# A transformer block in fp32 halves: the first token block's modulation, keys and queries reordered, and the feed-forward's norms and divisions moved to other chunks

## The chip, the core and the metric

The kernel runs on one core of one Trainium2 chip. A core has five engines, each with an instruction queue of its own: TensorE (PE, with weight loads shown as PEld), VectorE (DVE), ScalarE (ACT), GpSimd (POOL) and SyncE (SP), which here only issues DMAs. The metric is the device time of one execution in microseconds.

## The reference

One layer on x of 2048 tokens by 512 features, with a conditioning vector c of 512:

```
mod = silu(c) @ w_mod                       # six vectors of 512: sa, ca, ga, sb, cb, gb
h = layernorm(x) * (1 + ca) + sa
x = x + ga * (softmax attention of h, 32 heads of 16, wqkv, wo)
h = layernorm(x) * (1 + cb) + sb
x = x + gb * (gelu(h @ w1 + b1) @ w2 + b2)  # w1: 512 x 1792
```

## The kernel before

Wherever an fp32 product is needed, both operands are split into a rounded part (hi) and the rest (lo), and three matmuls are added up: hi·hi, lo·hi and hi·lo. `mm3` (L290 to L302) writes that order out for the four feature chunks of 128: eight matmuls that need only the hi of the second operand, then four that need its lo.

Tokens come in four blocks of 512 (b), features in four chunks of 128 (fc). Everything is issued in the order of the program text (`manual_schedule`), each engine in order; a wait on one instruction holds all behind it on that engine.

**Start.** SP issues the loads in this order: c, the four tiles of x's block 0, two whole 1 MB pieces of w_mod (1+ca and sa, L187, `load_wm` L137), block 0's share of the key and query weights (`load_w(0)`), and from L494 on the value weights, x's block 1 and the next weights. DVE takes mean and variance of block 0's rows (L236) and normalises them (L278). TensorE runs 22 products with the identity while it waits for data (`keep_warm`, L506, L510), then the modulation matmuls with ca (`mod_part`, L200), 12 of the 16 transposes of block 0, the matmuls with sa, and the last four transposes. ACT copies the modulation row out of PSUM (L213), four small matmuls turn it into columns (`mod_cols`, L216), DVE puts them into `modc`. `evac` (L260) then makes each feature chunk of hT: ACT scales and shifts the transposed chunk into an fp32 tile h (L262), DVE rounds it to hi (L263), DVE or POOL subtracts to give lo (L264). `split_w(0)` (L164) splits the first weights on DVE and POOL, `split_w(4)` the value weights on ACT, DVE and POOL.

**Loop over blocks** (L535 to L563). For block b: statistics of block b+1 (`ln1`), x of block b+2 is loaded, keys then queries of head group 0 are projected (`proj_qk`, 12 matmuls each into one PSUM bank of the ring "sc", four banks), block b+1's rows are normalised, `V_A[b][0]` value tiles are projected (`proj_v`, 12 matmuls each), block b+1 is transposed and evacuated, `V_A[b][1]` more value tiles, and for b < 2 the matmuls of the next modulation pair. After that come the remaining projections with row maxima beside them, and attention proper.

**Feed-forward** (from L869). 56 steps: four token blocks (qb) by 14 chunks of the 1792 features. Step i issues on each engine, in this order: the load of step i+4's weights, their split for step i+2 (`split_f`, L726: DVE rounds w1, POOL subtracts, DVE rounds w2, POOL subtracts), `ffn1(i)` (12 matmuls; ACT gelu, ACT rounds ghi, DVE subtracts glo, L906 to L910), `ffn2(i-1)` (12 matmuls into four accumulator banks, L927, the third of them needs glo of step i-1), and then what a table `plan` holds for this step. At the end of a token block `ffn2` also ends the block: DVE multiplies each accumulator by gb into one of three tiles y (L932), POOL adds it to x2 (L936; in the last block DVE does), SP stores. The table places, by step number: the attention output's division for blocks 2 and 3 (`o_norm`: a load of the reciprocals, then on DVE a multiply L781, a rounding L782 and a subtraction L783 for each feature chunk), the output projections (`o_proj`, 12 matmuls and a DVE add), and the second layer norm (`put_ln2`: statistics, `rows(t)` with two DVE instructions for a tile, L816 and L817, and transposes with four instructions a pair of chunks on ACT and DVE). In the loop's last two steps `ffn2` is left to the end (L1012 to L1017).

Of the kernel before, what the change touches and what calls it, by code (L numbers as in the profile page):

```python
# [7 lines left out]
F32 = mybir.dt.float32  # L8
# [16 lines left out]
NB = 4  # L25
# [27 lines left out]
def block_kernel(ctx: ExitStack, tc: tile.TileContext, x, wqkv, wo, w1, b1, w2, b2, c, w_mod, out):  # L53
# [28 lines left out]
    def bank():  # L82
        return ring("sc")
# [48 lines left out]
    sel_b = apool.tile([P, 2, P], F32, name="sel_b")  # L132
    ones = apool.tile([P, 2 * S // P], F32, name="ones")
    gp.memset(ones, 1.0)

    wm_r = w_mod.rearrange("(k p) n -> p k n", p=P)

    def load_wm(i, slot):
        sy.dma_start(halves[1][slot], wm_r[:, :, i * D : (i + 1) * D])
        return halves[1][slot]  # L140

    def x_tile(b, t):
# [10 lines left out]
    def load_w(k):  # L153
# [7 lines left out]
                sy.dma_start(raw[:, i], wq_r[:, i, 2 * D :])  # L161
        raws[k] = raw

    def split_w(k):  # L164
        raw = raws.pop(k)
        if k < 4:
            t = wslots[k % 2].rearrange("p a (b n) -> p (a b) n", n=P).rearrange("p (h w k) n -> p h w k n", h=2, w=2)
            for w in (1, 0):
                if k == 0:
                    ve.tensor_copy(t[:, 0, w], raw[:, w])  # L170
                elif k > 1:
                    gp.tensor_copy(t[:, 0, w], raw[:, w])
                else:
                    ac.activation(t[:, 0, w], raw[:, w], AF.Copy)
                eng = ve if k == 0 and w else gp
                eng.tensor_tensor(t[:, 1, w], raw[:, w], t[:, 0, w].bitcast(F32), op=ALU.subtract)
            w_hi[k], w_lo[k] = t[:, 0], t[:, 1]
        else:
            w_hi[k], w_lo[k] = vslots
            for i in range(KC):  # L180
                ac.activation(w_hi[k][:, i], raw[:, i], AF.Copy)
                eng = gp if i % 2 else ve
                eng.tensor_tensor(w_lo[k][:, i], raw[:, i], w_hi[k][:, i].bitcast(F32), op=ALU.subtract)
# [4 lines left out]
    load_w(0)  # L188


    ac.activation(s_c, c_c, AF.Exp, scale=-1.0)
# [8 lines left out]
    def mod_part(ps, i, wm):  # L200

        for k in range(KC):
            te.matmul(ps[32 * k : 32 * (k + 1)], s_m[:, i, k], wm[:, k], start=i == 0, stop=i == 1)

    def mod_rows(wms):
        ps = bank()
# [1 line left out]
            mod_part(ps, i, wms[i])  # L208
        return mod_copy(ps)

    def mod_copy(ps):
        r = apool.tile([P, D], F32, tag="h32", name="mrow", bufs=3)
        ac.activation(r, ps, AF.Copy)  # L213
        return r

    def mod_cols(v, r):  # L216

        ps = bank()
        for fc in range(KC):
            te.matmul(ps[:, fc * 2 : fc * 2 + 2], r[:, fc * P : (fc + 1) * P], sel[:, :2], start=True, stop=True)  # L220
        p2 = ps[:, : 2 * KC].rearrange("p (f i) -> p f i", i=2)
        ve.tensor_scalar(modc[:, v, :, 0], p2[:, :, 0], 1.0, None, op0=ALU.add)
        ve.tensor_copy(modc[:, v, :, 1], p2[:, :, 1])

    def mod_store(r):

# [77 lines left out]

    st = [ac]

    def proj_qk(b, k, w, fill=()):
        hi, lo = hT[b]
        ps = bank()
        mm3(ps, [w_hi[k][:, w, i] for i in range(KC)], [w_lo[k][:, w, i] for i in range(KC)],  # L310
            [hi[:, i] for i in range(KC)], [lo[:, i] for i in range(KC)], fill)
        parts = tpool.tile([P, 2, TB], FR, tag="parts", name="parts", bufs=5)
        pair = w and k < 2
        if k or pair and b % 2 == 0:
            raw = tpool.tile([P, TB], F32, tag="raw", name="raw", bufs=3)
            ac.activation(raw, ps, AF.Copy)
            if pair:
                k2[b % 2] = raw
        if k:
            gp.tensor_copy(parts[:, 0], raw)  # L320
            gp.tensor_tensor(parts[:, 1], raw, parts[:, 0].bitcast(F32), op=ALU.subtract)
        else:
            ac.activation(parts[:, 0], ps, AF.Copy)
            ve.tensor_tensor(parts[:, 1], ps, parts[:, 0].bitcast(F32), op=ALU.subtract)
        if pair and b % 2:
            pm = [tpool.tile([P, TB], F32, tag="pm", name="pm", bufs=1), k2[0]]
            pmh = [tpool.tile([P, 2, TB], FR, tag="parts", name="pmh", bufs=5) for _ in range(2)]
            if not k:
                for i, op in enumerate((ALU.add, ALU.subtract)):
                    ve.tensor_tensor(pm[i], ps, k2[0], op=op)  # L330
                    ac.activation(pmh[i][:, 0], pm[i], AF.Copy)

        def pair_store():
            for i in range(2):
                t0 = (b - 1 + i) * TB
# [18 lines left out]
    def proj_v(b, t, fill=()):  # L354
        hi, lo = hT[b]
        ps = bank()
        sl = slice(t * P, (t + 1) * P)
        mm3(ps, [hi[:, i, sl] for i in range(KC)], [lo[:, i, sl] for i in range(KC)],
            [w_hi[4][:, i] for i in range(KC)], [w_lo[4][:, i] for i in range(KC)], fill, late_b=False)
# [131 lines left out]
        return [] if left[u] else [max_rows(u)]  # L491


    load_w(4)  # L494
    load_x(1)
    load_w(1)
    sy.dma_start(one_d.rearrange("a (p f) -> (a p) f", p=P // 2), ones)
    xn = ln1(0)()
    for t in vst:
        gp.memset(t[:, :, 4 * VW :], 0.0)  # L500
        for j in range(4):
            gp.memset(t[:, :, j * VW + DH], 1.0)
    split_w(0)
    warm = bank_pv()

    def keep_warm(n):  # L506
        for i in range(n):
            te.matmul(warm[:, :P], ident, ident, start=True, stop=True)

    keep_warm(NWARM)  # L510
    ps = bank()
    mod_part(ps, 0, wms[0])
    ev = ln1_t(0, xn, lambda: mod_part(ps, 1, wms[1]))
    mrow = mod_copy(ps)
    keep_warm(5)
    mod_cols(0, mrow)
    ev()
    split_w(4)
# [12 lines left out]
    for b in range(NB):  # L531
# [6 lines left out]
            load_qm(0)  # L538
        if b + 1 < NB:
            rows = ln1(b + 1)  # L540
        if b + 2 < NB:
            load_x(b + 2)
        proj(proj_qk, b, 0, 1)
        if b == NB - 1:
            st[0] = sy
            rest()
            rest, st[0] = lambda: None, ac
            build_k(kts[0], kpm_d[0], 0, 0, 2 * TB)
            split_w(1)
            load_w(2)  # L550
        else:
            xn = rows()
        proj(proj_qk, b, 0, 0)
        if b == NB - 1:
            mod_store(mrow)
            break
        if b == 1:
            mod_cols(1, mrow)
        for _ in range(V_A[b][0]):
            proj(proj_v, *vitems.pop(0))  # L560
        ev = ln1_t(b + 1, xn)
        ev()
        for _ in range(V_A[b][1]):  # L563
# [421 lines left out]
    put_ln2(2, (0, 13), epool)  # L985
    put_ln2(3, (1, 11), fpool)
    for i in range(NI):
        qb, f = divmod(i, NF)
        if i + 4 < NI:
            load_f(i + 4)  # L990
        if i + 2 < NI:
            split_f(i + 2)
        ffn1(i)
        if i and i < NI - 2:
            ffn2([i - 1])
        for fn in plan.get((qb, f), []):
            fn()
    ffn2([NI - 3])
    ffn2([NI - 2, NI - 1])
    close(fcm)  # L1000
    close(kcm)

# [25 lines left out]
```

## Time and profile before

| | us |
|---|---|
| median of 3 runs (lowest, highest) | 1750.32 (1749.57, 1751.95) |
| the profiled execution's own time | 1751.07 |
| its span, first to last instruction | 1749.3 |
| PE busy | 1732.7 (99% of the span) |
| DVE, ACT, POOL busy | 1396.8, 1350.3, 320.2 |
| granted TensorE clock, mean | 0.998 |
| first block up to the first keys of block 1 | 0 to 41.45 |
| projections and row maxima, attention | to 1392 |
| feed-forward, from its first output projection | 1391.79 to the end |

Times on the trace are counted from the span's start. A row of the timeline gives start, duration, engine, line, operation, output and inputs with partitions and elements, and in brackets how long the engine had been idle and what ended it. An fp32 matmul counts as two instructions ("x44" for 22). A matmul row's duration includes its way through the array; the next one starts after about 0.227 us, which is the price of one 128x512 matmul in a stream.

### The profile page before, as it was taken

The numbers are of one execution on the slowest core, as the hardware profiler recorded it, in microseconds if no ns is written. First come the engines' busy times: TensorE is split into PE (matmuls) and PEld (weight loads), VectorE is DVE, ScalarE is ACT, GpSimd is POOL, SyncE is SP. The second block draws the span as 40 slices with busy tenths as digits, with TensorE's granted clock in tenths as the row PEclk, the third lists the DMA queues.
The fourth block names the chain that finished last, engine by engine and source line by source line (L and its number), as shares of the span: only waits on it lengthen the run. The fifth ranks groups of instructions, "written<-read, shape, count | busy, mean of one in ns | idle before, by whom it ended". The sixth has DMA issues, their size and how long they took to land.

```text
span 1749.3 us, 28886 instructions
## 1 busy us (share of the span) xinstructions
PE 1732.7 (99%) x10554; PEld 900.7 (51%) x10554; DVE 1396.8 (80%) x2553; ACT 1350.3 (77%) x2580; POOL 320.2 (18%) x347
## 2 busy tenths in 40 slices
PE   8999999999999999999999999999999999999998
PEld 6765554434343434343434343334333478788887
DVE  6579999898888888888888888888885295837453
ACT  3478888999999999999999999999999632212222
POOL 3205431010000000000000000000012154536462
PEclk9999999999999999999999999999999999999999
DMA  7777657611300501500510110111023164423331
GB/s 267 251 156 177 152 126 147 111 36 41 68 23 17 84 23 23 87 23 23 82 29 23 39 36 23 39 26 33 23 65 106 31 194 120 133 72 118 99 121 49
DMA packets 124098, 144.15 MB, mean 82 GB/s; under 512 B 38930, under 2 KB 72722, under 8 KB 122004
## 3 DMA queue, kind: packets, MB, share of 16 engines
q1 hardware_dynamic: 120644, 135.55, 31.6%
q10 hardware_dynamic: 3312, 6.76, 1.0%
q8 instruction: 83, 1.36, 0.4%
q14 instruction: 59, 0.48, 0.1%
HBM read 106.37 MB, written 35.87 MB: 81 GB/s over the span
## 4 chain that ended last, share of the span: by engine, by line
PE 93%; DVE 3%; DMA 1%; issue 1%; POOL 1%; SPq 0%; ACT 0%; ACTq 0%; DVEq 0%; POOLq 0%
PE pv L696 29%; PE mx L429 20%; PE sc L300 15%; PE sc L863 13%; PE mx L927 5%; PE mx L446 5%; PE pv L927 2%; PE sc L803 1%; PE mx L803 1%; DVE glo L910 0%; DMA wmod<-in_w_mod_dram 0%; POOL w2l L734 0%; DMA rb<-rden 0%; PE sc L257 0%; PE mx L257 0%
## 5 line engine op out<-in xcount | busy, mean ns | idle before, releaser
L864 ACT ACTIVATE p<-sc 128x512 f32<-128x512 f32 x2048 | 1054.7, 613 | 38.1 <-PE sc L863 12.5
L431 DVE TENSOR_REDUCE mxs<-mx 128x1 f32<-128x512 f32 x1472 | 927.7, 684 | 112.3 <-PE sc L863 87.3
L696 PE MATMUL pv<-p,vg 128*32 128x512 f32 x4096 | 546.0, 605 | 0.0
L863 PE MATMUL sc<-qst,kq 50*128 50x512 f32 x1024 | 284.2, 435 | 0.0
L863 PE MATMUL sc<-qst,kt 50*128 50x512 f32 x1024 | 282.0, 431 | 0.0
L429 PE MATMUL mx<-kq,qmx 48*128 48x512 f32 x768 | 261.7, 428 | 0.2
L429 PEld LDWEIGHTS mx<-kq,qmx 48*128 48x128 f32 x768 | 122.6, 184 | 228.6 <-DVE mxs L431 209.3
L429 PE MATMUL mx<-kt,qmx 48*128 48x512 f32 x704 | 240.0, 428 | 0.0
L906 ACT ACTIVATE g<-sc,b_c 128x512 f32<-128x512 f32 x56 | 38.6, 690 | 238.7 <-PE sc L300 230.6
L429 PEld LDWEIGHTS mx<-kt,qmx 48*128 48x128 f32 x704 | 113.4, 184 | 208.4 <-DVE mxs L431 190.6
L455 DVE CUSTOM_DVE_ANT_0 cp<-mx,cp 128x512 f32<-128x512 f32 x288 | 182.5, 687 | 25.9 <-PE mx L446 23.2
L468 POOL CAST m<-mn 128x16 fp32r<-128x16 f32 x32 | 6.3, 196 | 1018.4 <-DVE mn L462 1018.4
L696 PEld LDWEIGHTS pv<-p,vg 128*32 128x32 f32 x4096 | 81.1, 108 | 180.5 <-issue 168.9
L452 ACT ACTIVATE cp<-mx 128x512 f32<-128x512 f32 x288 | 151.6, 604 | 27.9 <-PE mx L446 27.0
L863 PEld LDWEIGHTS sc<-qst,kq 50*128 50x128 f32 x1024 | 125.5, 185 | 32.2 <-ACT p L864 23.7
L910 DVE TENSOR_TENSOR glo<-g,ghi 128x512 fp32r<-128x512 f32 x56 | 58.6, 1046 | 96.2 <-ACT ghi L909 96.2
L863 PEld LDWEIGHTS sc<-qst,kt 50*128 50x128 f32 x1024 | 125.6, 185 | 9.7 <-ACT p L864 3.1
L732 POOL TENSOR_TENSOR w1l<-w1r,w1h 128x512 fp32r<-128x512 f32 x56 | 76.8, 1371 | 154.0 <-DVE w1h L731 131.8
L446 PE MATMUL mx<-kt,qmx 48*128 48x512 f32 x576 | 103.9, 442 | 0.1
L734 POOL TENSOR_TENSOR w2l<-w2r,w2h 128x512 fp32r<-128x512 f32 x56 | 81.2, 1449 | 6.6 <-DVE w2h L733 6.2
L446 PEld LDWEIGHTS mx<-kt,qmx 48*128 48x128 f32 x576 | 54.6, 184 | 52.7 <-DVE mxf L455 26.4
L300 PE MATMUL sc<-hThi,w 128*128 128x512 f32 x256 | 77.7, 421 | 3.1 <-DVE hThi L263 3.1
(158 smaller groups left out, 1671.3 us busy)
## 6 DMA issues: line engine op xcount, KB each, us to landing
w1r<-in_B_w_dram SPq DMA_DIRECT2D x56, 256.0 KB
w2r<-in_B_w_dram SPq DMA_DIRECT2D x56, 256.0 KB
qk<-parts SPq DMA_DIRECT2D x25, 512.0 KB
qmx<-qk SPq DMA_DIRECT2D x192, 64.0 KB
qst<-qk SPq DMA_DIRECT2D x192, 64.0 KB
wmod<-in_w_mod_dram SPq DMA_DIRECT2D x6, 1024.0 KB
kq<-qk SPq DMA_DIRECT2D x24, 256.0 KB
kt<-qk SPq DMA_DIRECT2D x24, 256.0 KB
```

What stands on the lines that cost most here:

```text
L300: te.matmul(ps, p, q, start=i == 0, stop=i == len(terms) - 1)
L429: te.matmul(ps, qmx[u][rows, p, qc * P : (qc + 1) * P], kst[u // NB][rows, p, kr * TB : (kr + 1) * TB], start=True, stop=True)
L431: ve.tensor_reduce(mxs[u][:, p, a, qc, kr : kr + 1], ps, axis=AX.X, op=ALU.max, negate=True)
L446: te.matmul(ps, qmx[u][rows, p, qc * P : (qc + 1) * P], kpm[u // NB][rows, p, t0 : t0 + TB], start=True, stop=True)
L452: ac.activation(vabs[n, a], ps, AF.Abs)
L455: ve.tensor_tensor_reduce(v, ps, v, -0.5, 3.0e38, ALU.add, ALU.min, mxs[u][:, p, a, qc, r : r + 1])
L696: te.matmul(cur_pv[0][32 * j : 32 * (j + 1)], vg[g][:, kc, j * VW : j * VW + 32], pt.pop((s, j)), start=kc == 0, stop=kc == NKC - 1)
L732: gp.tensor_tensor(alo, a, ahi.bitcast(F32), op=ALU.subtract)
L734: gp.tensor_tensor(blo, b, bhi.bitcast(F32), op=ALU.subtract)
L863: te.matmul(ps, k[r0 : r0 + KX, p, kc * P : (kc + 1) * P], q[r0 : r0 + KX, p], start=True, stop=True)
L864: ac.activation(pb, ps, AF.Exp, scale=SCALE)
L927: te.matmul(acc[qb][t], p[:, sl], q, start=f == 0 and n == 0, stop=f == NF - 1 and n == 2)
```

## The change

Four things are changed; everything else is the same text.

1. The two w_mod pieces come in halves of 256 columns: SP issues the first halves of both (in four loads of two row chunks each), then the first weights, then the second halves, the value weights and x's block 1. x's block 2 is loaded right behind the first block's work and ahead of the next w_mod pieces; the weights of head group 1 are loaded in block 1's turn. The memsets of the value tiles stand at the start.
2. `first_block` replaces `ln1_t(0)`, `split_w(0)`, `split_w(4)`, `mod_part` and the projections of block 0's keys and queries. The modulation is done for feature chunks 0 and 1, then for 2 and 3, and keys and queries advance side by side. ACT rounds the first weights and makes hi directly from PSUM (`put`), and h once more for lo.
3. `V_A[0]` is (3, 0): three value tiles ahead of block 1's transposes, none behind. The first value tile uses the other order of `mm3`.
4. In the feed-forward, steps of the table move, and the last step before the end joins two into one group of three.

```
-V_A = ((1, 2), (1, 1), (0, 1))
+V_A = ((3, 0), (1, 1), (0, 1))
...
     load_x(0)
-    wms = [load_wm(1, 0), load_wm(0, 1)]
+    for i in range(2):
+        for k in (0, 2):
+            load_wm(1 - i, i, 0, HD, k, k + 2)
+    wms = halves[1]
     load_w(0)
+    for i in range(2):
+        load_wm(1 - i, i, HD, D)
+    load_w(4)
+    load_x(1)
...
+        keep_warm(NWARM)
+        mod_part(mod, 0, wms[0], 0, HD)
+        mod_part(mod, 1, wms[1], 0, HD)
+        mrow = mod_copy(mod, None, 0, HD)
+        for w in (1, 0):
+            ac.activation(w_hi[0][:, w], raw[:, w], AF.Copy)
+        keep_warm(3)
+        tr(0)
+        mod_cols(0, mrow, cols, 0, 2)
+        for t in range(1, 4):
+            tr(t)
+        for w in (1, 0):
+            sub(w_lo[0][:, w], raw[:, w], w_hi[0][:, w])
+        put(hi[:, 0], 0)
+        put(hi[:, 1], 1)
+        keep_warm(2)
+        mm("hh", 0)
+        mod_part(mod, 0, wms[0], HD, D)
+        mm("hh", 1)
+        mm("lh", 0, 1)
+        mod_part(mod, 1, wms[1], HD, D)
+        hs = {}
+
+        def lower(fc):
+            hs[fc] = apool.tile([P, TB], F32, tag="h32", name="h32", bufs=3)
+            put(hs[fc], fc)
+            sub(lo[:, fc], hs[fc], hi[:, fc])
+            return lambda: mm("hl", fc)
+
+        lower(0)()
+        hl1 = lower(1)
+        mod_copy(mod, mrow, HD, D)
+        mod_cols(0, mrow, cols, 2, 4)
+        hl1()
+        for fc in (2, 3):
+            put(hi[:, fc], fc)
+        hl = [lower(fc) for fc in (2, 3)]
+        keep_warm(3)
+        mm("hh", 2, 3)
+        mm("lh", 2, 3)
+        for f in hl:
+            f()
...
-    put(0, 7, lambda: o_load(3))
+    put(0, 9, lambda: o_load(3))
     for t in range(4):
         for i, d in enumerate((0, 1, 1, 2)):
-            put(0, 1 + t + d, lambda t=t, i=i: o_norm(2, t)[i]())
-            put(0, 8 + t + d, lambda t=t, i=i: o_norm(3, t)[i]())
-        put(0, 8 + t, lambda t=t: [f() for f in o_proj(2, t)])
-        put(1, 5 + t, lambda t=t: [f() for f in o_proj(3, t)])
+            put(0, 3 + t + d, lambda t=t, i=i: o_norm(2, t)[i]())
+            put(*divmod(10 + t + d, NF), lambda t=t, i=i: o_norm(3, t)[i]())
+        put(0, 9 + t, lambda t=t: [f() for f in o_proj(2, t)])
+        put(1, 6 + t, lambda t=t: [f() for f in o_proj(3, t)])
     put(1, 1, lambda: load_x2(3, x2[0]))
     put_ln2(1, (0, 1), fpool)
-    put_ln2(2, (0, 13), epool)
-    put_ln2(3, (1, 11), fpool)
+    put_ln2(2, (1, 3), epool)
+    put_ln2(3, (1, 12), fpool)
...
-        if i and i < NI - 2:
+        if i and i < NI - 3:
             ffn2([i - 1])
...
-    ffn2([NI - 3])
-    ffn2([NI - 2, NI - 1])
+    ffn2([NI - 4])
+    ffn2([NI - 3, NI - 2, NI - 1])
```

In `first_block`, `put(dst, fc)` is ACT's scale and shift of chunk fc, `mm("hh" | "lh" | "hl", fcs)` one matmul for keys and one for queries per chunk, `tr(t)` the four transposes of token tile t. Behind what is shown it rounds the value weights on DVE (two chunks) and ACT (two) and subtracts on DVE (two) and POOL (two).

More of the change, by code (lines that the diff above doesn't have):

```diff
@@ L134, in block_kernel, with load_wm @@
     gp.memset(ones, 1.0)
+    for t in vst:
+        gp.memset(t[:, :, 4 * VW :], 0.0)
+        for j in range(4):
+            gp.memset(t[:, :, j * VW + DH], 1.0)
     wm_r = w_mod.rearrange("(k p) n -> p k n", p=P)
-    def load_wm(i, slot):
-        sy.dma_start(halves[1][slot], wm_r[:, :, i * D : (i + 1) * D])
+    HD = D // 2
+    def load_wm(i, slot, c0=0, c1=D, k0=0, k1=KC):
+        sy.dma_start(halves[1][slot][:, k0:k1, c0:c1], wm_r[:, k0:k1, i * D + c0 : i * D + c1])
         return halves[1][slot]
@@ L162, in load_w, with w_parts @@
         raws[k] = raw
+    def w_parts(k):
+        t = wslots[k % 2].rearrange("p a (b n) -> p (a b) n", n=P).rearrange("p (h w k) n -> p h w k n", h=2, w=2)
+        w_hi[k], w_lo[k] = t[:, 0], t[:, 1]
     def split_w(k):
         raw = raws.pop(k)
[L166 to L183, printed above, removed]
+        w_parts(k)
+        for w in (1, 0):
+            if k > 1:
+                gp.tensor_copy(w_hi[k][:, w], raw[:, w])
+            else:
+                ac.activation(w_hi[k][:, w], raw[:, w], AF.Copy)
+            gp.tensor_tensor(w_lo[k][:, w], raw[:, w], w_hi[k][:, w].bitcast(F32), op=ALU.subtract)
     sy.dma_start(c_c, c.rearrange("a (k p) -> p (a k)", p=P))
     load_x(0)
-    wms = [load_wm(1, 0), load_wm(0, 1)]
+    for i in range(2):
+        for k in (0, 2):
+            load_wm(1 - i, i, 0, HD, k, k + 2)
+    wms = halves[1]
     load_w(0)
+    for i in range(2):
+        load_wm(1 - i, i, HD, D)
+    load_w(4)
+    load_x(1)
+    sy.dma_start(one_d.rearrange("a (p f) -> (a p) f", p=P // 2), ones)
     ac.activation(s_c, c_c, AF.Exp, scale=-1.0)
@@ L198, in block_kernel, with mod_part @@
     gp.tensor_copy(sel_b, sel[:, :2, None].to_broadcast([P, 2, P]))
-    def mod_part(ps, i, wm):
+    def mod_part(ps, i, wm, c0=0, c1=D):
         for k in range(KC):
-            te.matmul(ps[32 * k : 32 * (k + 1)], s_m[:, i, k], wm[:, k], start=i == 0, stop=i == 1)
+            te.matmul(ps[32 * k : 32 * (k + 1), c0:c1], s_m[:, i, k], wm[:, k, c0:c1], start=i == 0, stop=i == 1)
     def mod_rows(wms):
@@ L209, in mod_rows, with mod_copy, mod_cols @@
         return mod_copy(ps)
-    def mod_copy(ps):
-        r = apool.tile([P, D], F32, tag="h32", name="mrow", bufs=3)
-        ac.activation(r, ps, AF.Copy)
-        return r
-    def mod_cols(v, r):
-        ps = bank()
-        for fc in range(KC):
+    def mod_copy(ps, r=None, c0=0, c1=D):
+        if r is None:
+            r = apool.tile([P, D], F32, tag="h32", name="mrow", bufs=3)
+        ac.activation(r[:, c0:c1], ps[:, c0:c1], AF.Copy)
+        return r
+    def mod_cols(v, r, ps=None, f0=0, f1=KC):
+        if ps is None:
+            ps = bank()[:, : 2 * KC]
+        for fc in range(f0, f1):
             te.matmul(ps[:, fc * 2 : fc * 2 + 2], r[:, fc * P : (fc + 1) * P], sel[:, :2], start=True, stop=True)
-        p2 = ps[:, : 2 * KC].rearrange("p (f i) -> p f i", i=2)
-        ve.tensor_scalar(modc[:, v, :, 0], p2[:, :, 0], 1.0, None, op0=ALU.add)
-        ve.tensor_copy(modc[:, v, :, 1], p2[:, :, 1])
+        p2 = ps.rearrange("p (f i) -> p f i", i=2)
+        ve.tensor_scalar(modc[:, v, f0:f1, 0], p2[:, f0:f1, 0], 1.0, None, op0=ALU.add)
+        ve.tensor_copy(modc[:, v, f0:f1, 1], p2[:, f0:f1, 1])
     def mod_store(r):
@@ L305, in block_kernel, with first_block, keep_warm, tr @@
     st = [ac]
-    def proj_qk(b, k, w, fill=()):
+    def first_block(tiles):
+        hi = hpool.tile([P, KC, TB], FR, name="hThi0")
+        lo = hpool.tile([P, KC, TB], FR, name="hTlo0")
+        hT[0] = hi, lo
+        raw, vr = raws.pop(0), raws.pop(4)
+        w_parts(0)
+        w_hi[4], w_lo[4] = vslots
+        warm = bank_pv()
+        cols = warm[:, P : P + 2 * KC]
+        mod = bank()
+        xT = [bank_mx() for _ in range(KC - 1)] + [bank()]
+        acc = {w: bank() for w in (1, 0)}
+        def keep_warm(n):
+            for i in range(n):
+                te.matmul(warm[:, :P], ident, ident, start=True, stop=True)
+        def tr(t):
+            for fc in range(KC):
+                te.transpose(xT[fc][:, t * P : (t + 1) * P], tiles[t][:, fc * P : (fc + 1) * P], ident)
+        def put(dst, fc):
+            ac.activation(dst, xT[fc], AF.Identity, scale=modc[:, 0, fc, 0:1], bias=modc[:, 0, fc, 1:2])
+        def mm(kind, *fcs):
+            for fc in fcs:
+                for w in (1, 0):
+                    p, q = {"hh": (w_hi, hi), "lh": (w_lo, hi), "hl": (w_hi, lo)}[kind]
+                    te.matmul(acc[w], p[0][:, w, fc], q[:, fc], start=kind == "hh" and fc == 0,
+                              stop=kind == "hl" and fc == KC - 1)
+        def sub(dst, a, b, eng=ve):
+            eng.tensor_tensor(dst, a, b.bitcast(F32), op=ALU.subtract)
+        keep_warm(NWARM)
+        mod_part(mod, 0, wms[0], 0, HD)
+        mod_part(mod, 1, wms[1], 0, HD)
+        mrow = mod_copy(mod, None, 0, HD)
+        for w in (1, 0):
+            ac.activation(w_hi[0][:, w], raw[:, w], AF.Copy)
[4 more added lines that the diff above has]
+            tr(t)
+        for w in (1, 0):
+            sub(w_lo[0][:, w], raw[:, w], w_hi[0][:, w])
[26 more added lines that the diff above has]
+            f()
+        for i in range(KC):
+            if i < 2:
+                ve.tensor_copy(w_hi[4][:, i], vr[:, i])
+            else:
+                ac.activation(w_hi[4][:, i], vr[:, i], AF.Copy)
+        for i in range(KC):
+            sub(w_lo[4][:, i], vr[:, i], w_hi[4][:, i], gp if i > 1 else ve)
+        return acc
@@ L308, in proj_qk @@
+    def proj_qk(b, k, w, fill=(), ps=None):
         hi, lo = hT[b]
-        ps = bank()
-        mm3(ps, [w_hi[k][:, w, i] for i in range(KC)], [w_lo[k][:, w, i] for i in range(KC)],
-            [hi[:, i] for i in range(KC)], [lo[:, i] for i in range(KC)], fill)
+        if ps is None:
+            ps = bank()
+            mm3(ps, [w_hi[k][:, w, i] for i in range(KC)], [w_lo[k][:, w, i] for i in range(KC)],
+                [hi[:, i] for i in range(KC)], [lo[:, i] for i in range(KC)], fill)
         parts = tpool.tile([P, 2, TB], FR, tag="parts", name="parts", bufs=5)
@@ L352, in proj_qk, with proj_v @@
         return rest
-    def proj_v(b, t, fill=()):
+    def proj_v(b, t, fill=(), late_w=False):
         hi, lo = hT[b]
@@ L358, in proj_v @@
         mm3(ps, [hi[:, i, sl] for i in range(KC)], [lo[:, i, sl] for i in range(KC)],
-            [w_hi[4][:, i] for i in range(KC)], [w_lo[4][:, i] for i in range(KC)], fill, late_b=False)
+            [w_hi[4][:, i] for i in range(KC)], [w_lo[4][:, i] for i in range(KC)], fill, late_b=late_w)
         v = vst[(b * 4 + t) % len(vst)]
@@ L491, in next_max @@
         return [] if left[u] else [max_rows(u)]
[L494 to L518, printed above, removed]
+    first = first_block(ln1(0)())
+    load_x(2)
     wms = [load_wm(4, 0), load_wm(3, 1)]
@@ L540, in block_kernel @@
             rows = ln1(b + 1)
-        if b + 2 < NB:
+        if b and b + 2 < NB:
             load_x(b + 2)
-        proj(proj_qk, b, 0, 1)
+        proj(proj_qk, b, 0, 1, (), None if b else first[1])
+        if b == 1:
+            load_w(1)
         if b == NB - 1:
@@ L550, in block_kernel @@
             load_w(2)
-        else:
+        elif b:
             xn = rows()
-        proj(proj_qk, b, 0, 0)
+        proj(proj_qk, b, 0, 0, (), None if b else first[0])
+        if b == 0:
+            xn = rows()
         if b == NB - 1:
@@ L559, in block_kernel @@
         for _ in range(V_A[b][0]):
-            proj(proj_v, *vitems.pop(0))
+            proj(proj_v, *vitems.pop(0), (), len(vitems) == 15)
         ev = ln1_t(b + 1, xn)
```

## The prediction

> **What bounds the kernel now.** The page gives TensorE 99% of the span, and its chain of work that ended last is 93% PE. So I asked for TensorE's waits: all of them lie at the start and in the feed-forward, none in between.
>
> ```profile
> PE mx L927 <- DVE glo L910: 3.4, 4, 2.3
> PE sc L300 <- DVE hThi L263: 3.1, 3, 1.6
> PE sc L203 <- DMA wmod<-in_w_mod_dram: 2.6, 1, 2.6
> ```
>
> Totals in us, times, longest. From 93 to 1392 us no wait of PE is listed, so what is gained ahead of it moves all that follows earlier, one for one. The timeline of PE at the start:
>
> ```profile
> 11.04 1.06 PE L203 MATMUL sc<-wmod,s_m 128*32 128x512 f32 x8 [2.60 <-DMA wmod<-in_w_mod_dram]
> 12.03 2.71 PE L257 MATMUL mx<-ident,xin 128*128 128x128 f32 x12
> ...
> 20.27 0.73 PE L300 MATMUL sc<-hThi,w 128*128 128x512 f32 x2 [1.60 <-DVE hThi L263]
> ...
> 23.70 0.73 PE L300 MATMUL sc<-hThi,w 128*128 128x512 f32 x2 [1.17 <-DVE hThi L263]
> ...
> 27.64 1.07 PE L300 MATMUL sc<-hTlo,w 128*128 128x512 f32 x4
> ...
> 41.45 2.11 PE L300 MATMUL sc<-hThi,w 128*128 128x512 f32 x8
> ```
>
> Block 0's keys and queries end at 28.71; block 1's keys begin at 41.45. Between 11.04 and 41.45 PE is held up by hT (the gaps shown) and by a slow clock. The table by windows (PE, PEld, DVE, ACT, POOL busy, then granted clock, DMA share, GB/s):
>
> ```profile
> 12.00:14.00 2.00, 2.00 (x14) 1.83 (x11) 0.51 (x2) 0.00 (x0) 0.00 (x0) 0.55 1.14 331
> 14.00:16.00 2.00, 2.00 (x12) 0.54 (x10) 1.40 (x3) 0.00 (x0) 0.00 (x0) 0.60 1.06 385
> ...
> 1511.00:1512.00 1.00, 1.00 (x4) 0.80 (x3) 0.97 (x2) 0.00 (x0) 0.50 (x1) 0.50 1.14 238
> ```
>
> After an idle stretch the clock is halved for some 3.5 us: once at 12.2, once at 1510.7, behind the longest wait of the feed-forward. There the timelines of DVE, POOL and PE read:
>
> ```profile
> 1502.65 0.69 DVE L932 TENSOR_TENSOR y<-pv,gb_b 128x512 f32<-128x512 f32 x1 [1.90 <-POOL x2a L936]
> 1503.26 0.90 DVE L816 TENSOR_SCALAR xn_b<-x2b,mv,rs 128x512 f32<-128x512 f32 x1
> 1504.19 1.67 DVE L817 TENSOR_TENSOR x2b<-x2b,b_b 128x512 f32<-128x512 f32 x1
> ...
> 1508.61 1.75 DVE L910 TENSOR_TENSOR glo<-g,ghi 128x512 fp32r<-128x512 f32 x1
> ```
> ```profile
> 1501.33 5.68 POOL L936 TENSOR_TENSOR x2a<-x2a,y 128x512 f32<-128x512 f32 x4
> ```
> ```profile
> 1510.42 0.62 PE L927 MATMUL mx<-w2h,glo 128*128 128x512 f32 x1 [2.25 <-DVE glo L910]
> ```
>
> At the end of token block 0 (step 14) the fourth y waits for POOL; then the norm's rows run at 1.5 to 1.7 us where 0.54 and 0.69 are their durations beside an idle POOL; glo of step 15 comes 2.25 us late, and the next ten matmuls take 1510.42 to 1514.39 = 3.97 us instead of 2.27.
>
> **Part A, the first block.** Start of the chain: the first halves of both modulation pieces are 1 MB behind x, the place in the queue that the first whole piece had: 11.0. Their runs are 1 KB instead of 2 KB. No row has 1-KB runs; near 12 to 13.5 us, when the first weights (512-B runs) pass, the rows show 301 to 330 GB/s against 385 around them. I take half that loss on 1 MB, 0.2 us (ends: 0 and 0.5): 11.2. The Trainium skill, DMA: Bandwidth & Descriptors, Specifications, puts line rate at 512 B and more; by it this term would be 0, though the rows dip at just that size.
> From there, by rows: modulation half of the x8 row, 0.53 (11.75); ACT's copy of half a row, nothing shown, between 0 and the 0.60 of a whole row, taken 0.4 (12.15), beside it on PE 3 products of 0.26 and 4 transposes (0.45); 2 of the 4 column matmuls (0.95 for four): 0.48; 12 transposes at 0.11: 1.3, so 14.7. ACT makes hi 0 and 1 (0.79, then 0.7 each): 15.2 and 15.9. PE: 8 matmuls at 0.227 and two modulation halves of 0.5, 2.8 from 15.25: 18.1. Copy 0.4, columns 0.5, DVE's modc 0.3: 19.4. ACT then makes hi 2, 3 and h 2, 3, four at 0.7: 22.1; DVE's last lo 0.69: 22.8; the last two matmuls: **23.4, where before had 28.7.** The first weights' split (ACT 2x0.6, DVE 2x0.69) and the eight extra ACT passes lie inside this chain as far as shown; the three extra warming products lie in waits.
> Given back: (a) the value weights are now split later. DVE and POOL took 2.4 and 3.0 us for two subtractions each; the first value tile needs them in its last four matmuls: about 0.6. (b) The third value tile needs the bank of the first keys, freed by a DVE subtraction (L324) that queues behind block 1's statistics (4x0.8): until 30.0, so 0.6. Value tiles end at 23.4 + 3x2.72 + 1.2 = 32.8. (c) Transposes 1.65 without the wait of before (the x12 row at 31.34 took 2.31 against 1.47 later), modulation pair 1.87: 36.3. But block 1's hT, which had two value tiles as cover, has only this pair now: from the first bank to the last lo ACT, DVE and POOL took 33.49 to 39.53. Starting at 33.35 it ends at 39.4, and the keys wait 0.4 and 0.3 for it. They end at 39.8; before, 41.45 + 2.97 = 44.4. **A: -4.6.** Moved loads: x of block 2 goes ahead of the next modulation pieces, 3 MB issued by 19.5, landing by about 30 at the shown 385 GB/s, used at 34.5; the weights of group 1 are used after 74. Both cost nothing.
> The clock: before, 2.6 us of idle ahead of 12.2 halved it, the 1.60 at 18.7 did not. Now the idle is about 0.9 and 1.3 with a half-size modulation between. Taken: no loss (nearer the 1.60 that cost nothing); the other end +1.1.
>
> **Part B, early steps of the feed-forward.** Division and rows no longer meet in steps 2 and 3, so the wait of 0.82 at 1434.55 goes; in steps 5 to 8 the division meets the norm's transposes, and the 0.15 at 1453 grows to about 0.5. Taken -0.4 (ends -1.0, +0.5).
>
> **Part C, step 14.** The norm's rows leave; the division of block 3 comes in their place: three DVE instructions instead of four. But the square root of the norm (POOL, 1.12) and its statistics are gone from step 13, so POOL's adds start right behind the first y, as at the next block ends (the fourth y waits 0.65 and 0.21 there). glo of step 15 is then ready at about 1507.9 on the old clock, needed at 1508.2. The wait and the lost clock go, 2.25 + 1.70; I keep 0.25 for what is left. -3.7. By the Trainium skill, TensorE: Matmul & The Clock Gate, Why this matters for your kernels, only gaps over about 3 us lower the clock, and then this part would be -2.0; the trace has the lowered clock behind 2.25, and decides.
>
> **Part D, step 28.** put_ln2(3) goes from 25 to 26, so rows 2 and 3 fall in step 28, behind block 1's y: the order that was bad at step 14. The fourth y ends at 1595.61 there; with the 7.1 us that step 14 took from it to the end of glo, glo of step 29 is ready at 1602.7 and needed at 1601.6 (the transposes that stood in step 29 go to 30): +1.1. Ends: 0, and 2.25 + 1.70 = 3.95 as at step 14.
>
> **Part E, the end.** The last three steps share the last group, so the accumulators end 9 matmuls (2.04) apart instead of 6 and DVE keeps up: behind PE's end stand one y and one add, 1.4, instead of 1.86 (1744.29 to 1746.15). -0.5. The last ghi (three buffers, four alive) waits on ACT for the step-52 group; ghi and glo then lie beside six matmuls (1.36). Ends: -0.9, and +1.4 if PE must wait for them.
>
> **Sum:** -4.6 - 0.4 - 3.7 + 1.1 - 0.5 = -8.1. The profiled execution, 1751.07 (span 1749.3 and 1.77 around it), becomes 1743.0; the median before is 0.75 below it, so 1742.2.
>
> **Rivals.**
> 1. The clock is lost at the start (+1.1) and step 28 repeats step 14 whole (+2.85 over D): 1746.2. For it: the same queue order; against: the transposes no longer stand in step 29. The Trainium skill, TensorE: Matmul & The Clock Gate, Part 1, says the activity window runs free, so that the point varies; no single trace shows that. Chance 0.2.
> 2. The returns (a) and (b) and D do not come, since statistics and splits overlap better than queued in a row: -2.3, and the copies of half rows are quicker, -0.6: 1739.3. Chance 0.15.
> 3. Block 1's hT chain, without its cover, is the new bound in full: hi and lo late by 2.5 where I have 0.7, and (a), (b) double (+1.2), +3.0, with +0.6 elsewhere: 1745.8. For it, the 5.2 to 6 us of that chain; against, in before's block 2 one value tile and less hid it. Chance 0.12.
> 4. **Slower:** the halves with 1-KB runs crawl. Every us that they land later moves the whole chain. To end 0.2% above before they must land 11.6 us later (3.5 + 8.1), 1 MB at some 75 GB/s: 1754. At 301, the lowest row with shorter runs, it is 0.7. Chance 0.04.
> Forecast as above: 0.49.
>
> **Numbers.** A measurement of this kernel tells about 0.2%, 3.5 us, from no change: faster is below 1746.8. Forecast, 2, and most of 1 and 3 are faster: 0.84. The rest of 1 and 3: same 0.12; slower 0.04. The range takes in the ends of A (-4.6 - 1.2 for the returns - 0.2 for the loads = -6.0; -4.6 + 1.1 for the clock + 0.3 for the loads + 0.2 for the copy = -3.0) and of D: 1738.5 to 1747.0; forecast, 1, 2 and 3 lie in it, and their far sides with 4 are the 2 in 10 left out.
>
> **What will show it.** Right: first modulation near 9.5 and 11.2; keys and queries done near 23.4; block 1's keys starting near 36.3 with short waits; no 2.25 us wait at the end of token block 0; a wait near 1 us on glo in step 29. Wrong: PE waiting for hT of block 1 for over 2 us; a wait on glo with a granted clock of 0.50 in steps 15 or 29; a start of modulation behind 12.

## The result, and the profile after

The changed kernel takes 1745.43 us (median, 1744.65 to 1746.25) where the kernel before takes 1750.23 on the same chip (1749.57 to 1751.95): a ratio of 0.9967 [0.9958, 0.9977], 4.8 us faster. The forecast was 1742.2. The profiled execution takes 1745.77 with a span of 1744.0, 5.3 below the span of before. Four marks of the two traces say where these 5.3 lie:

| stretch, us | before | after | difference | forecast |
|---|---|---|---|---|
| start to the first row-max product (L543 in after) | 93.45 | 91.41 | -2.04 | A: -4.6 |
| to the first output copy of attention (osb, ACT) | 229.76 | 229.59 | -0.17 | 0 |
| first to last output copy | 1068.69 | 1069.63 | +0.94 | 0 |
| last output copy to the end | 357.40 | 353.37 | -4.03 | B to E: -3.5 |

So the feed-forward did a little better than forecast and the first block gave under half. TensorE's waits in the changed kernel (engine, line, what it waited for; us in total, times, longest):

```profile
PE mx L1005 <- DVE glo L988: 1.5, 1, 1.5
PE sc L309 <- DVE wv L396: 1.4, 2, 0.8
...
PE sc L210 <- DVE xin L287: 0.2, 1, 0.2
```

The wait for modulation weights (2.6) and those for block 0's hT are gone, and of the four for glo one is left. New is a wait for wv, the rounded value weights. (The 0.2 ahead of the second modulation half stands as a wait for DVE; the traces of C1 and E9 below put the same wait down to the load of wmod.) PE's timeline at the start:

```profile
10.16 1.33 PE L210 MATMUL sc<-wmod,s_m 128*32 128x256 f32 x8 [0.20 <-DVE xin L287]
11.42 0.94 PE L333 MATMUL pv<-ident 128*128 128x128 f32 x6
...
15.05 0.73 PE L346 MATMUL sc<-hThi,w 128*128 128x512 f32 x2
...
22.92 1.29 PE L346 MATMUL sc<-hTlo,w 128*128 128x512 f32 x4
25.00 0.47 PE L309 MATMUL sc<-wv,hThi 128*128 128x512 f32 x1 [0.79 <-DVE wv L396]
...
26.33 0.51 PE L309 MATMUL sc<-wv,hThi 128*128 128x512 f32 x1 [0.63 <-DVE wv L396]
...
34.43 1.47 PE L266 MATMUL mx<-ident,xin 128*128 128x128 f32 x12
...
38.12 2.44 PE L309 MATMUL sc<-hThi,w 128*128 128x512 f32 x8
40.40 1.31 PE L309 MATMUL sc<-hTlo,w 128*128 128x512 f32 x4
41.55 1.99 PE L309 MATMUL sc<-hThi,w 128*128 128x512 f32 x8
...
47.99 2.15 PE L266 MATMUL mx<-ident,xin 128*128 128x128 f32 x12
```

Block 0's keys and queries end at 24.21 (22.92 + 1.29; 28.71 before), 4.5 earlier, but block 1's keys begin at 38.12 instead of 41.45, only 3.3 earlier: in between lie the two waits for value weights. Then 2.44 stands for block 1's keys where such a row takes 1.99 without a stall (the queries at 41.55), and the transposes of block 2 take 2.15 instead of 1.47. The clock, from the table by windows, did not drop:

```profile
13.00:14.00 1.00, 1.00 (x11) 1.00 (x11) 0.82 (x4) 0.24 (x1) 0.00 (x0) 1.00 1.11 359
```

(1.00 ahead of DMA share and GB/s is the granted clock, 0.50 at this place before.) The value weights, in the timelines of DVE and of POOL:

```profile
22.06 1.36 DVE L350 TENSOR_TENSOR hTlo<-h,hThi 128x512 fp32r<-128x512 f32 x2 [2.18 <-ACT h L340]
23.34 2.93 DVE L396 CAST wv<-vraw 128x512 fp32r<-128x512 f32 x2
26.19 1.28 DVE L350 TENSOR_TENSOR wv<-vraw,wv 128x512 fp32r<-128x512 f32 x2
```
```profile
23.29 2.69 POOL L350 TENSOR_TENSOR wv<-vraw,wv 128x512 fp32r<-128x512 f32 x2 [13.86 <-ACT wv L398]
```

Two roundings take 2.93 us on DVE, while POOL runs its two subtractions. A rounding of this size takes 0.42 elsewhere (the median of L809); its longest, 1.51 at 1596.32, also runs beside a POOL subtraction (L812, 1595.81 to 1597.54). In the feed-forward, behind token block 0 and behind token block 1 (DVE, then PE):

```profile
1498.06 0.69 DVE L1010 TENSOR_TENSOR y<-pv,gb_b 128x512 f32<-128x512 f32 x1 [0.21 <-POOL x2a L1014]
...
1503.57 1.77 DVE L988 TENSOR_TENSOR glo<-g,ghi 128x512 fp32r<-128x512 f32 x1
```
```profile
1596.45 0.50 PE L1005 MATMUL mx<-w2h,glo 128*128 128x512 f32 x1 [1.52 <-DVE glo L988]
```

At step 14 the fourth y waits 0.21 for POOL instead of 1.90, and PE no longer waits for glo. At step 29 it waits 1.52; the products behind it run on at 0.39, so the clock held. POOL's adds of step 14 now start about 0.1 behind the first y (1496.74), before about 1.8 behind it (1501.33). At the end, PE's last product and DVE's last add:

```profile
1739.16 0.39 PE L1005 MATMUL pv<-w2h,glo 128*128 128x512 f32 x1
```
```profile
1740.32 0.69 DVE L1014 TENSOR_TENSOR x2a<-x2a,y 128x512 f32<-128x512 f32 x1
```

The last add ends 1.46 behind PE's end, 1.86 before.

### The profile page after: what moved, and what is told of

Its sections match the earlier page's. It is cut to its first block, busy times and chain, and to the rows that moved or that the text cites. A ratio compares the mean times of both kernels' runs of the same rounds, so it can differ in the third digit from the quotient of the medians.

```text
span 1744.0 us, 28927 instructions
## 1 busy us (share of the span) xinstructions
PE 1733.8 (99%) x10576; PEld 900.0 (52%) x10576; DVE 1397.3 (80%) x2554; ACT 1353.1 (78%) x2585; POOL 316.6 (18%) x344
## 4 chain that ended last, share of the span: by engine, by line
PE 95%; DVE 3%; ACT 0%; DMA 0%; issue 0%; SPq 0%; POOL 0%; ACTq 0%; DVEq 0%
PE pv L774 29%; PE mx L526 20%; PE sc L309 16%; PE sc L941 13%; PE mx L1005 6%; PE mx L543 5%; PE pv L1005 2%; PE sc L881 2%; PE mx L881 1%; PE sc L266 0%; DVE glo L988 0%; DMA wmod<-in_w_mod_dram 0%; DVE xin L287 0%; DVE mxs L528 0%; PE sc L210 0%
## 5 line engine op out<-in xcount | busy, mean ns | idle before, releaser
L543 PE MATMUL mx<-kt,qmx 48*128 48x512 f32 x576 | 103.6, 442 | 0.1
L812 POOL TENSOR_TENSOR w2l<-w2r,w2h 128x512 fp32r<-128x512 f32 x56 | 82.4, 1472 | 6.6 <-DVE w2h L811 6.2
L543 PEld LDWEIGHTS mx<-kt,qmx 48*128 48x128 f32 x576 | 54.2, 184 | 52.8 <-DVE mxf L552 28.0
L309 PE MATMUL sc<-kt,w1h 128*128 128x512 f32 x224 | 73.8, 391 | 0.0
```

Of the source, the lines that this page charges most:

```text
L309: te.matmul(ps, p, q, start=i == 0, stop=i == len(terms) - 1)
L543: te.matmul(ps, qmx[u][rows, p, qc * P : (qc + 1) * P], kpm[u // NB][rows, p, t0 : t0 + TB], start=True, stop=True)
L812: gp.tensor_tensor(blo, b, bhi.bitcast(F32), op=ALU.subtract)
```

## Experiments

Each is the changed kernel with the edit shown, unless said otherwise, measured beside the kernel before on its own chip. "Front" is the time from the end of the first modulation to the first row-max product: with half loads the modulation ends (the next product starts) between 10.1 and 11.4 by execution, mostly as its weights land, and front leaves that out (in E2 the modulation is the old one, so no front is given). "FF" runs from the last output copy to the end.

| kernel | us | before there | ratio, interval | first mod. ends | front | FF |
|---|---|---|---|---|---|---|
| changed | 1745.43 | 1750.23 | 0.9967 [0.9958, 0.9977] | 11.42 | 79.99 | 353.37 |
| E1 front alone | 1748.87 | 1750.22 | 0.9995 [0.9986, 1.0003] | 10.40 | 80.00 | 357.20 |
| E2 feed-forward alone | 1747.86 | 1750.22 | 0.9989 [0.998, 0.9998] | | | 354.67 |
| E3 early split | 1742.26 | 1750.22 | 0.996 [0.9948, 0.9973] | 10.95 | 77.98 | 353.48 |
| E4 rows at step 27 | 1742.55 | 1750.22 | 0.9962 [0.995, 0.9975] | 10.62 | 79.99 | 351.61 |
| E7 = E3 + E4 | 1741.41 | 1750.81 | 0.9951 [0.9937, 0.9965] | 10.76 | 78.00 | 351.56 |
| E10 = E7 + cover | 1741.6 | 1750.81 | 0.9951 [0.9938, 0.9963] | 10.25 | 78.28 | 351.62 |
| E8 whole loads | 1750.8 | 1750.81 | 1.0001 [0.9992, 1.0009] | 14.27 | 81.14 | 353.55 |
| E9 norm back | 1752.14 | 1750.81 | 1.0009 [1.0, 1.0018] | 11.30 | 79.98 | 360.28 |
| C1 changed, again | 1744.54 | 1750.5 | 0.9967 [0.9955, 0.998] | 10.68 | 79.95 | 353.39 |
| E11 low parts on DVE | 1743.19 | 1750.5 | 0.996 [0.9947, 0.9974] | 10.10 | 79.01 | 353.41 |
| C2 = E7, again | 1740.71 | 1750.5 | 0.9948 [0.9935, 0.996] | 10.90 | 77.99 | 351.56 |

**E1 and E2, the two halves of the change.** E1 puts all moved lines of the feed-forward's table and its last groups back (two lines are shown); E2 is the kernel before with only these moved.

```diff
-    put_ln2(2, (1, 3), epool)
-    put_ln2(3, (1, 12), fpool)
+    put_ln2(2, (0, 13), epool)
+    put_ln2(3, (1, 11), fpool)
...
```

> The changed kernel with the feed-forward's table and its last group put back as before: parts A alone. Theory T1 (the front's gain is what the changed trace shows at the first row-maximum matmul, 93.45 to 91.41, and nothing behind eats it): -2.0 us against before. Rival R1 (the attention stage takes back about 0.75 to 0.9 us of it whatever chip it runs on, as the drift from -2.2 at 323 us to -1.3 at 1391 us in the two traces would have it): -1.2. In its trace the lead over before stays constant from 100 to 1390 us by T1 and shrinks by R1.

> The kernel before with the feed-forward's new table and last group: parts B to E alone. T1: from the first output projection to the end 353.4 us as in the changed trace (357.5 before), so -4.1 in all, and the time up to 1391 us as before. By R1, which puts a loss of 0.8 on the new front, likewise -4.1 here. If the feed-forward's gain came from where the front leaves the phases of the engines, it would be under -3.

By the medians E1 is 1.35 below before and E2 2.4, together 3.7 of the 4.8. E1's interval reaches from -2.5 to +0.5 and holds the -2.0 of T1, the -1.2 of R1 and no change, so its time decides nothing and the traces must. E1's first row-max product comes at 90.40 (its modulation ended 1.0 earlier than in the changed kernel's profile, its front is the same), and attention takes 1068.66 in E1 and 1068.69 in E2. So the 0.94 more of attention is neither half's: R1 falls. The same kernel, E7 and C2, took 1069.33 and 1068.74; it varies by execution, from a cause that stays open.

E2 missed its forecast: -4.1 lies outside its interval (-3.5 to -0.4), and its FF is only 2.7 shorter than before's; under 3 was to mean that the gain hangs on the new front. Up to the last add, though, FF takes 350.45 in E2, 350.38 in the changed kernel and 354.25 before, so the gain of 3.8 is there without the new front; the last output then lands 4.2 behind that add, in the changed kernel 3.0. Whether other executions of E2 land as late, no trace shows. E2 also keeps the old start:

```profile
10.46 1.06 PE L203 MATMUL sc<-wmod,s_m 128*32 128x512 f32 x8 [2.09 <-DMA wmod<-in_w_mod_dram]
```
```profile
12.00:13.00 1.00, 0.93 (x6) 0.93 (x6) 0.02 (x1) 0.00 (x0) 0.00 (x0) 0.53 1.19 315
```

Behind a wait of 2.09 its granted clock is 0.53 to 0.50.

**E3 and E11, why the value weights are late.** E3 moves DVE's roundings and subtractions up, ahead of the products of the second half (and ahead of POOL's subtractions); E11 leaves the order and takes POOL's subtractions away from beside them.

```diff
+        for i in range(2):
+            ve.tensor_copy(w_hi[4][:, i], vr[:, i])
+        for i in range(2):
+            sub(w_lo[4][:, i], vr[:, i], w_hi[4][:, i])
         hl1()
         for fc in (2, 3):
             put(hi[:, fc], fc)
...
-            sub(w_lo[4][:, i], vr[:, i], w_hi[4][:, i], gp if i > 1 else ve)   # E11
+            sub(w_lo[4][:, i], vr[:, i], w_hi[4][:, i], ve)                    # E11
```

> The changed kernel, with DVE's two roundings and two subtractions of the value weights moved up into the stretch where DVE is idle (19.9 to 22.1 us), ahead of the last two lo parts. Theory T2: the first value tile waits 0.79 and 0.63 us for these roundings, which take 2.93 us because POOL's subtractions hold them up; without it value tiles start near 24.1, block 1's keys end 2.2 us earlier, and all behind them too: -2.2 against the changed kernel, -7 against before. Rival R2: block 1's rows or its hT (DVE and ACT) are late anyway, and the wait only moves there: -0.5 or less against the changed kernel. A wait for the value weights' load in place of these would show as DVE idle until a DMA near 20 us.

> The changed kernel, but the subtractions for the value weights of chunks 2 and 3 run on DVE too, behind its own two, and no longer on GpSimd; the order is else untouched. T8 (the two DVE roundings took 2.93 us instead of 0.8 because GpSimd's subtractions ran beside them): the roundings take 0.75 to 0.85, both waits for value weights (0.79 and 0.63) go though DVE now has two subtractions more, and everything behind moves up by 1.4 to 1.9; 1743.7 us, 0.999 of the changed kernel. R8 (the roundings are slow because of what they read or of where they stand, or the split as such comes too late): the waits stay at 1.4 or grow by the 1.3 of DVE's two further subtractions; the time is that of the changed kernel or up to 1.3 more.

DVE's and PE's timelines of E3:

```profile
19.32 0.75 DVE L386 CAST wv<-vraw 128x512 fp32r<-128x512 f32 x2
```
```profile
22.45 1.29 PE L346 MATMUL sc<-hTlo,w 128*128 128x512 f32 x4
23.58 0.39 PE L309 MATMUL sc<-wv,hThi 128*128 128x512 f32 x1
...
31.97 1.47 PE L266 MATMUL mx<-ident,xin 128*128 128x128 f32 x12
```

and of E11:

```profile
22.02 0.75 DVE L396 CAST wv<-vraw 128x512 fp32r<-128x512 f32 x2
22.69 2.49 DVE L350 TENSOR_TENSOR wv<-vraw,wv 128x512 fp32r<-128x512 f32 x4
...
28.50 1.28 DVE L421 TENSOR_TENSOR parts<-sc,parts 128x512 fp32r<-128x512 f32 x2
```
```profile
29.24 2.13 PE L309 MATMUL sc<-wv,hThi 128*128 128x512 f32 x8 [0.71 <-DVE parts L421]
```

In both the two roundings take 0.75 and no product waits for them. From the end of the queries the three value tiles take 8.23 in E3 (23.74 to 31.97) and 10.22 in the changed kernel (24.21 to 34.43): 1.99 for the late split, and the front is 2.01 shorter. E11 settles the reason: at the same place in the queue, without POOL beside them, the roundings are quick; R8 falls. By the Trainium skill, SBUF — State Buffer, Who interferes with whom, a VectorE instruction in a two-port mode waits for the whole of a GpSimd instruction that already holds their shared ports; the rows agree (1.47 each beside POOL's 1.35, 0.375 alone). But E11 gained 0.98 of front and 1.35 in all, not 1.4 to 1.9: the third tile finds its PSUM bank still held by DVE's subtraction behind block 1's statistics, 0.71. This is the wait of term (b), but E11 makes it itself: DVE's four subtractions take 2.49 where two took 1.28, and all that stands behind them on DVE, that bank too, comes 1.2 later. With 1.2 less the bank would be free about 0.5 ahead of the tile (an estimate from these rows), and in E3, whose tiles are as early, no such wait is listed.

**E10, the cover of block 1's hT.** E7 with one value tile behind the transposes again.

```diff
-V_A = ((3, 0), (1, 1), (0, 1))
+V_A = ((2, 1), (1, 1), (0, 1))
```

> E7, and one of block 0's three value tiles goes behind the transposes of block 1 again (2 tiles, transposes, 1 tile, modulation, keys of block 1). T5 (the late hT of block 1 still costs what its stalls show in E3's trace): the first keys of block 1 lose the stalls within their products (3.43 from their start to the next products' in E3, 3.19 without a stall as the next ones run, plus what the start waits) and the transposes of block 2 lose 0.68 (2.15 instead of 1.47), so -0.7 to -1.2 against E7. R5: two value tiles are too short a cover for DVE's statistics: the rows of block 1 come at 27.5 to 29.4, the transposes at 29.2, and what the keys gain the transposes lose: within 0.3 of E7.

```profile
34.99 2.12 PE L309 MATMUL sc<-hThi,w 128*128 128x512 f32 x8
...
44.29 1.48 PE L266 MATMUL mx<-ident,xin 128*128 128x128 f32 x12
...
57.69 2.57 PE L266 MATMUL mx<-ident,xin 128*128 128x128 f32 x12 [0.54 <-DVE xin L287]
```

The stalls of block 1's keys and of block 2's transposes (1.48 instead of 2.15) do go. But block 2's keys now stall, and block 3's transposes wait 0.54 for their rows and run at 2.57 (2.36 in E7). The front is 0.28 longer than E7's, the time 0.2 above it. No gain, as R5 said, though the loss came a block later than R5 had it: two tiles were cover enough for block 1, and the lead that PE gained was taken back by the next rows from DVE.

**E8, whole loads.** What do the half loads bring?

```diff
-        for k in (0, 2):
-            load_wm(1 - i, i, 0, HD, k, k + 2)
+        load_wm(1 - i, i)
...
-    for i in range(2):
-        load_wm(1 - i, i, HD, D)
```

> The changed kernel, but each modulation weight comes in one load of 1 MB ahead of the projection weights, as before the change; the products stay in two halves of columns and side by side. T6 (the front's gain is the earlier landing of the first halves): the first modulation ends at about 15.3 instead of 11.5 as in the kernel before, every product behind it moves by 3 to 4 us, and the first row-max product comes at 94.5 to 95.5, 1 to 2 later than in the kernel before; 1748.5 to 1749.5 us. R6 (the gain is the order of the products, side by side, with the earlier landing hidden): the first row-max product stays within 1 of the changed kernel's 91.4 and the time within 1 of 1745.4.

```profile
13.26 1.08 PE L207 MATMUL sc<-wmod,s_m 128*32 128x256 f32 x8 [2.14 <-DMA wmod<-in_w_mod_dram]
14.27 1.65 PE L330 MATMUL pv<-ident 128*128 128x128 f32 x6
```
```profile
14.00:15.00 1.00, 1.00 (x7) 0.73 (x4) 0.00 (x0) 0.61 (x2) 0.00 (x0) 0.50 1.06 376
```

The first row-max product comes at 95.41, 4.0 later than in the changed kernel and 2.0 later than before: 2.85 from the landing (14.27 - 11.42) and 1.15 behind it, where the clock is 0.50 again (the row at 14.27 takes 1.65, in the changed kernel 0.94). T6 holds for the place of this product; the time lies 1.3 above T6's range. Without the early halves the rest of the new first block, with its late split of the value weights, is slower than the old one.

**E4 and E9, the two block ends of the feed-forward.** E4 puts the rows of block 3's norm back to step 27; E9 puts block 2's norm back to step 13, where the changed kernel now divides.

```diff
-    put_ln2(3, (1, 12), fpool)
+    put_ln2(3, (1, 11), fpool)     # E4
-    put_ln2(2, (1, 3), epool)
+    put_ln2(2, (0, 13), epool)     # E9
```

> The changed kernel with the last norm one step earlier again (25 instead of 26), so that its rows do not follow a block end. Theory T3: the wait of 1.52 us for glo in step 29 is due to these rows, held up by POOL's adds; it goes, and nothing else: -1.5 against the changed kernel, -6.3 against before. Rival R3: the statistics in step 24 to 25 or the transposes in step 29 bring a wait of their own there: 0 to -0.7.

> The changed kernel, but block 2's norm begins at step 13 again, where the changed kernel now has the divisions of block 3. T7 (the statistics and rows of the norm at a block's end hold DVE and GpSimd, and with them y and glo): a wait for glo of at least the 2.25 of the kernel before comes back at step 14 or 15, and with the divisions on the same engine up to 6, with TensorE's clock dropping behind it (1.7 us in the kernel before): 4 to 8 us slower than the changed kernel, 1749.5 to 1753.5. R7 (the divisions' old place had been the cause): less than 1 us slower.

E4's FF is 1.8 shorter, and of the waits for glo 0.2 is left (1.5 in the changed kernel): T3 holds, and the cost of part D was avoidable. E9 is 6.1 slower than the changed kernel (1.33 above before instead of 4.8 below). Its DVE, PE and table of windows:

```profile
1499.87 0.69 DVE L1010 TENSOR_TENSOR y<-pv,gb_b 128x512 f32<-128x512 f32 x1 [1.93 <-POOL x2a L1014]
```
```profile
1509.53 0.79 PE L1005 MATMUL mx<-w2h,glo 128*128 128x512 f32 x1 [4.43 <-DVE glo L988]
```
```profile
1510.00:1515.00 5.00, 5.00 (x13) 3.84 (x13) 4.93 (x8) 0.00 (x0) 1.61 (x2) 0.50 0.63 224
```

The fourth y waits 1.93 for POOL as before the change, the rows queue behind the divisions, glo is 4.43 late, and the clock falls to 0.50. T7 holds: it is the norm at the block's end that cost the time there.

**E7, C1 and C2, both mended places.**

> Both mended places together: the split of the value weights ahead of the second keys' products (E3) and the rows of block 3's norm one step earlier (E4). T2 and T3 (two separate stalls on PE, some 1550 us apart, each of which sets the end by itself): the gains add up, -1.5 to -2.5 for the split and -1.8 for the rows against the changed kernel, so 1741.1 us give or take 0.6, no wait for value weights, waits for glo of at most 0.3 in all. Rival: the two share a cause, or the slack of a later stage swallows one of them: the time stays at that of the better one alone, 1742.3.

> The changed kernel once more, as the measure for the two others on the same chip: 0.9967 of the kernel before give or take 0.001. If the stage of attention takes 1068.7 here (first to last output copy), the 1069.6 of the first profile belonged to that execution; if 1069.6, to the changed kernel or to the chip, which the two others then tell apart.

> Both mended places (E7) again, beside the changed kernel on one chip. Two separate gains, 2.0 for the split and 1.8 for the rows of step 27 by the traces so far: 3.5 to 4.2 us below the changed kernel of this call. Rival: a later stage takes part of it back in most executions, though not in the profiled one: under 3 us.

Front and FF of E7 show both gains whole (78.00 and 351.56), and on one chip C2 is 3.83 us below C1 (1740.71 against 1744.54; 1740.62 to 1742.66 and 1744.29 to 1744.95): two separate gains. It is 0.9948 [0.9935, 0.996] of the kernel before, the best kernel here. C1's attention took 1069.53; as E7 and C2 differ by 0.59 there with one code, this tells nothing of the change.

## Why the prediction was right and wrong

Right: faster, inside the range, and by the steps named, though part A gave under half. The profiled execution came 2.8 us above its forecast of 1743.0: 2.6 from part A and 0.9 from attention, less 0.5 from the feed-forward and 0.2 between.

- **A, start of the chain.** Forecast for the two halves 9.5 and 11.2; they ran at 9.30 and 10.16 in the profiled execution, and the modulation ended at 11.42 for 11.75. What the runs of 1 KB cost is small: from 7 to 9 us the table by windows shows 349 and 364 GB/s (397 and 395 before, but 367 and 358 with the whole loads of E8), and rival 4 is out. No lost clock, as taken.
- **A, keys and queries done:** 23.4 forecast, 24.21 measured, +0.8, though it began 0.3 early. The eight matmuls and two modulation halves took 3.38 (15.05 to 18.43) for 2.85; so the second columns' modc ended at 19.9 instead of 19.4, and DVE's last lo at 23.42 instead of 22.8.
- **A, (a): the step that failed.** "About 0.6" for the value weights' split; it measured 1.99 (E3). The forecast priced subtractions at rows of before and looked at the low parts alone; what came late were the two roundings ahead of them, held up by POOL (E11).
- **A, (b):** 0.6 forecast; no wait came, neither in the changed kernel nor in E3, where (a) is gone. E11's 0.71 is of its own making. (a) alone was 0.8 above both forecasts together. Value tiles and what stands between them and the keys took 0.3 more than forecast.
- **A, block 1's keys:** begun at 38.12 for 36.3, ended at 41.71 (40.40 + 1.31) for 39.8. The stalls in them were as forecast, 0.57 (3.43 from their start to the queries', 2.86 before) for 0.7. What the sum left out is the next turn of the same chain: block 2's transposes stall 0.68 for their rows, which DVE makes in 3.87 beside two subtractions of POOL (L443), where block 1's took 1.92 (an experiment without that company was not run). E10 shows that this is no local gap: cover one block, and the next pays.
- Together: +0.8, +0.8 and +0.3 up to the keys, +0.7 behind them, -4.6 becomes -2.0; the marks give -2.04. This lies outside part A's own ends, -6.0 and -3.0. That the total still lies in the range is in part luck: the range was wide for a lost clock at the start and for the whole of step 14 again at step 28, and neither came, while the terms that missed had narrower ends.
- **B:** -0.4 forecast; the waits of 0.82, 0.18 and 0.15 all went, -1.15. The 0.5 for division beside transposes did not come.
- **C:** -3.7 forecast, -3.95 measured: the wait of 2.25 and the 1.70 of clock both went whole, and POOL's adds start right behind the first y, as said. E9 brings wait and clock loss back with the norm. By the Trainium skill, TensorE: Matmul & The Clock Gate, Why this matters for your kernels, only gaps above about 3 us lower the clock; the runs disagree: it fell behind single waits of 2.09 (E2), 2.25 (before) and 4.43 (E9) and behind 1.52 and 2.14 close together (E8), not behind 1.52 at step 29.
- **D:** +1.1 forecast, +1.52 measured, in the place named and without a loss of clock.
- **E:** -0.5 forecast; the last add 0.40 closer to PE's end, and the landing behind it about 0.1 shorter.
- **One for one:** what the front gained did move all behind it in E1 and E4 (attention 1068.66 and 1068.69, before 1068.69); the 0.94 more in the changed kernel's profile came in others too and has no cause shown.

Of the rivals, 3 gave 1745.8, near the time measured, and half of it came: (a) more than tripled, but the keys of block 1 did not wait 2.5, they waited as the forecast had it. Rival 1 asked for a lost clock at the start, which did not come; rival 2 for the returns to vanish, and (a) grew.

## What to carry to other kernels

When work moves off a chain, price each instruction in the company it will have, not only at its row: a 0.4 us rounding on VectorE was 1.5 beside a GpSimd subtraction, and moving it 4 us up or taking GpSimd's work away mended it. A repair that moves work can bring a wait of its own: E11's two further subtractions on VectorE held back a PSUM bank for 0.7. And where each block hands its lead to the next, follow a gain through two or three blocks before counting it.

## What the runs showed beyond that

- The landing of the first modulation weights, and with it the start of the work, moves by some 1.2 us between executions of the same loads (first modulation ended between 10.25 and 11.42; at 10.10 in E11, where the warming products and not the loads came last).
- Attention took 1068.7 in all four profiles of the chip that ran E1 to E4 and 1069.0 to 1069.6 in the four of the chip that ran E7 to E10; the chip of C1, E11 and C2 shows both (1069.53, 1068.68, 1068.74). The chip alone does not decide it, and the cause stays open.
- The kernel before went from 1748.16 to 1754.9 over all its executions, and its slow ones have the lower mean clock: beside E7 to E10, a mean of 1748.8 for the four at 0.999 and of 1754.1 for the two at 0.995. That is not all of the scatter: E10, whose profile shows no drop, went from 1740.49 to 1743.47.
- POOL's subtraction suffers less: 1.35 beside DVE's roundings, 1.29 in the median of L812, though up to 1.75 there (1.73 at 1595.81, beside DVE's glo and the long rounding named above).
